# Half of h by seven products in the q/k stage, five probability tiles a head summed by DMA, output by seven products

## The chip, the cores and the metric

One core of a Trainium2 chip runs the kernel. The metric is device time in microseconds (us), the median of timed runs. TensorE (PE) multiplies matrices, VectorE (DVE) and ScalarE (ACT) work on tiles in SBUF and PSUM, GpSimd (POOL) on tiles in SBUF, and the queues of SyncE (SP), ACT and POOL issue transfers to 16 shared DMA engines. Each engine runs its own instructions in a fixed order and waits on semaphores of the others.

## The reference

With S = 2048 tokens, D = 1024, H = 32 heads of 32, F = 3584:

```python
xn = _layernorm(x)
q, k, v = heads(xn @ wqkv)
p = softmax(einsum("bhqd,bhkd->bhqk", q, k) * 32 ** -0.5)
s = merge(einsum("bhqk,bhkd->bhqd", p, v)) @ wo
h = xn @ w1 + b1
g = silu((h * tanh(softplus(h))) @ w2)       # Dense -> Mish -> Dense
return x + s * g
```

All is float32. Products that need its precision are made from two parts of each operand, high and low, in a reduced-precision float format: a product of tiles is three matmuls (high x high, high x low, low x high; `THREE`).

## The kernel before

The program runs in four stages.

1. **v stage.** The rows of x are normalised, transposed and split into high and low (`xc`); PE makes v and stores it in DRAM. Beside it the first 7 of w1's 28 column tiles are split (`w1_early`) and stored in `w1s`.
2. **q/k stage** (L798). Sixteen jobs; each makes one 128-row tile of q and one of k for two of the four 512-column chunks of x, by seven products in place of eight: with sums of quarter blocks of the weights (`w_sum`, on POOL) and of x (`t_half`), each product is 12 matmuls, so a job is 84. Three PSUM banks a job collect the products, DVE adds between them (`after`), ACT and DVE split the results (`out_`), and ACT's queue stores them.
3. **Inner stage.** Four streams are woven on PE by a planner (`Plan`) which, while the program is written, simulates the engines with fixed durations and writes each instruction where it would be ready, by due times (`due`, `key`) and a table of leanings. `s_stream`: scores for the row maxima (L920, one head ahead; DVE reduces them). `t_stream`: for every head h and key tile kt (16 a head, `T` counts them all) four transposed scores (L1007), which ACT turns into a probability tile `p` of 128x2048 by Exp; one of `PS` = 7 buffers. POOL adds the 16 tiles into `z` (L1036), 15 adds a head. `product` (L1054) multiplies groups of 6, 5 and 5 probability tiles with v; these matmuls use PE's columns in four parts, 32 wide, and a stretch of them is called a stay. `norm` sums z over partitions by four such matmuls (`zp`, L1080), inverts it and stores the head in DRAM (`ot`). `h_stream` (L1213): per chunk c and column tile f of w1, 24 matmuls make h, 112 tiles of 128x512 in all; `mish` takes DVE and ACT through the activation; a whole split w1 tile (1 MB) is loaded to one of two buffers for each. `y_stream` (L1303) multiplies the activations with w2 and DVE adds into `yacc`. In the first chunk w1 and w2 are split on the way by ACT and POOL, and kept.
4. **Output** (L1402). 768 matmuls with wo. The first chunk's eight banks are done in two halves, rows k = 0..3 of wo's eight (heads 0 to 15) first. `end` multiplies with silu(y) and adds x.

A tile p is given back when both its add and its product are done (`p_done`).

Of the kernel before, what the change touches and what calls it, by code (L numbers as in the profile page):

```python
# [28 lines left out]
SLOW, UNTIL = 1.25, 700.0  # L29

W2_Q = 0
NS = H * NT
HK = KT // 2

MM, PV = 0.228, 0.86

GROUPS, YB = (6, 5, 5), 2

LEAD, LATE = 5, 4.0

PS, ACTS, W2S, Y0, Y1 = 7, 3, 5, 0.6, 0.17

AHEAD, BEHIND = 1.5, 1
# [9 lines left out]
LEAN = ("11875111088588544715468766661886741604280263056046486663654100588"  # L53
        "24308444562028442608686254255866647666488105044664767708017872000")
# [35 lines left out]
class Plan:  # L90
# [6 lines left out]
    SEM, SWITCH, LAND, RATE = 0.07, (0.25, 0.13), 2.0, 0.25e6  # L97
# [25 lines left out]
    def ready(self, op):  # L123
        when = 0.0
        for o in op.need:
            if o is not None:
                if o.end is None:
                    return None
                when = max(when, o.end + self.SEM)
        if op.late and not self.col:  # L130
            when += op.late
        for name in op.take:
            if not self.rings[name]:
                return None
            when = max(when, min(self.rings[name])[0] + self.SEM)
        return when
# [14 lines left out]
    def do(self, op, when):  # L151
# [11 lines left out]
        else:  # L163
            op.end = start + took
# [66 lines left out]
def body(ctx: ExitStack, tc: tile.TileContext, x, wqkv, wo, w1, b1, w2, out):  # L231
# [17 lines left out]
    w1s = [dram.tile([P, 2, KT, P], F32R, name=f"w1s{i}") for i in range(FT)]  # L249
# [10 lines left out]
    nc.vector.memset(one, 1.0)  # L260
    zero = consts.tile([P, 1], F32, name="zero")
# [38 lines left out]
    def w1_tile(name):  # L300
        return w1p.tile([P, 2, KT, P], F32R, tag="w1", name=name, bufs=2)
# [132 lines left out]
    def split_w(w, raw, job=False):  # L434
        for half in range(2):
            r = slice(half * 4, half * 4 + 4)
            if job:
                nc.gpsimd.tensor_copy(w[:, 0, r], raw[:, r])
            else:
                copy(w[:, 0, r], raw[:, r])  # L440
            low(nc.gpsimd if job else nc.vector, w[:, 1, r], raw[:, r], w[:, 0, r])
# [4 lines left out]
    def w1_early():  # L446
# [3 lines left out]
        if f > 1:  # L450
            move(w1s[f - 2], early_w1.pop(f - 2)[1])
        if f < W1_V:
            raw = vp.tile([P, KT, P], F32, tag="x", name=f"w1e{f}", bufs=XB)
            nc.sync.dma_start(raw, w1[:, f * P:(f + 1) * P].rearrange("(k p) f -> p k f", p=P))
            early_w1[f] = [raw, None]
        if 0 < f <= W1_V:
            raw, _ = early_w1[f - 1]
            early_w1[f - 1][1] = w = w1_tile(f"w1p{f - 1}")
            split_w(w, raw, True)
# [75 lines left out]
    nc.sync.dma_start(bias1, b1.rearrange("(f p) -> p f", p=P))  # L535

    PAIRS = ((2, 3), (0, 1))
    A11, S2, A12, S3, S1, A22, S4 = range(7)
    NQ = 2 * KT
    raws, sums, pieces = {}, {}, {}  # L540

    def q_load(q, tiles, halves=range(2)):
        raws[q] = tiles
        for half in halves:
            col = half * D + q % KT * P
            nc.sync.dma_start(tiles[half], wqkv[:, col:col + P].rearrange("(k p) f -> p k f", p=P))
# [9 lines left out]
    EARLY = {(6, 0): [(7, 0)], (6, 2): [(7, 2)], (6, 4): [(7, 1)], (7, 4): [(8, 0)]}  # L556
# [4 lines left out]
    def piece(n, eng):  # L561
        q, i = SEQ[n]
        if n % 2 == 0:
            pieces["tile"] = w1_tile(f"wq{n // 2}")
        w = pieces[n] = pieces["tile"][:, :, n % 2 * HK:n % 2 * HK + HK]
# [169 lines left out]
    def load_w1(n):  # L735
        w1t[n] = w1_tile(f"w1_{n}")
        move(w1t[n], w1s[n % FT])
# [30 lines left out]
    def ring_of(q):  # L768
        if q < KT + 2:
# [5 lines left out]
    def out_(q, half, chunk_, src):  # L775
        st = sp.tile([P, 2, 512], F32R, tag="qst", name=f"qst{q}_{half}_{chunk_}", bufs=4)
        dst = (qs, ks)[half][q % KT].rearrange("h p n -> p h n")[:, :, chunk_ * 512:(chunk_ + 1) * 512]
# [9 lines left out]
    def product(n):  # L787
        q, i = SEQ[n]
        bank_, e = banks_.setdefault(q, {}), es.setdefault(q, {})
        c0, c1 = PAIRS[q // KT]  # L790
        w, xx = pieces.pop(n), X[q // KT][i]
# [31 lines left out]
    for n, (q, i) in enumerate(SEQ):  # L823
        after = product(n)
        for m in (n + 2, n + 3) if n >= 2 and n % 2 == 0 else ():
            if m >= 7 * NQ:
                continue
            piece(m, nc.vector if q < 11 or m % 2 else nc.gpsimd)
            q_, i_ = SEQ[m]
            if i_ == A22:  # L830
                if q_ == 9:
# [8 lines left out]
            if i_ in ((A12, A22) if q_ else (A22,)) and q_ + 2 < NQ and q_ != 7:  # L840
# [5 lines left out]
        since = n - SEQ.index((KT - 1, 0))  # L846
        for _ in range(T_SPLITS.get(since, 0)):
            t_splits.pop(0)()
        if (q, i) >= (11, 2):
# [5 lines left out]
        if since in (6, 9):  # L855
            q_load(9, ring_of(9), (since == 9,))
        for k in B_LOADS.get(since, ()):
            move(X[1][6][:, :, k], xs[1][:, :, HK + k])
        if i == 0 and q == 10:
            load_head(0)  # L860
        if i == 3 and q == 14:
            load_head(1)
        if i == 5 and q == NQ - 1:
            load_w1(0)
# [13 lines left out]
    for name, n in (("b", 7), ("s", S_B), ("t", T_B), ("d", D_B), ("o", 1), ("p", PS), ("z", 1), ("e", 1), ("r", 1), ("on", 1),  # L878
                    ("act", ACTS), ("w1", 2), ("w2", W2S), ("w2r", 1), ("xc0", 1), ("xc1", 1), ("v", 2), ("mx", 2), ("nm", 2), ("hl", 1),
# [15 lines left out]
    total = 2 * 4 * NS * MM + NC * FT * 48 * MM + NS * PV  # L895
    slot = total / NS

    def due(T):
# [3 lines left out]
        return UNTIL * SLOW + (t - UNTIL) * (total - UNTIL * SLOW) / (total - UNTIL)  # L902
# [33 lines left out]
    def m_chain(h, first, n, maxes, tiles):  # L936
# [23 lines left out]
        def r6(at):  # L960
# [3 lines left out]
            if h == 0:  # L964
                load_w1(1)
# [11 lines left out]
    exps, adds, uses = {}, {}, {}  # L977
# [9 lines left out]
    def p_done(T, by):  # L987

        uses.setdefault(T, []).append(by)
        if len(uses[T]) == 2:  # L990
            plan.give("p", max(o.end for o in uses[T]))

    def t_stream():
        pts = {}
        for T in range(NS):
# [29 lines left out]
            if kt:  # L1025
                add(T, pts)
            if kt in group_of:
                product(T, pts, group_of[kt])

    def add(T, pts):  # L1030
        h, kt = divmod(T, NT)

        def emit(at):
            if kt == 1:
                zs[h] = att.tile([P, S], F32, tag=f"z{at['z']}", name=f"z{h}")
            nc.gpsimd.tensor_tensor(zs[h], pts[T - 1] if kt == 1 else zs[h], pts[T], ALU.add)  # L1036

        def then(o):
            if kt == 1:
                p_done(T - 1, o)  # L1040
            p_done(T, o)
# [519 lines left out]
```

## Time and profile before

| | |
|---|---|
| median of 3 timed runs | 3362.53 us (3361.49 to 3362.98) |
| span of the profiled execution, first to last instruction | 3358.0 us |
| v stage, q/k stage, inner stage, output | 0 to 200, to 521.5, to 3179.1, to 3358 us |
| busy: PE, DVE, ACT, POOL | 3345.8, 2510.8, 2056.5, 2524.7 us |
| granted PE clock | 1.00 |
| DMA | 501.56 MB, 149 GB/s on the mean |

The stages' borders are the first starts of their lines. A row of the groups reads: line, engine, operation, output<-inputs, shapes, count | busy us, mean ns of one | idle time of the engine just before them and what ended it. Matmuls are pipelined, so the duration of one is longer than the distance between two. Times in the timeline count from the start of the span.

### The profile page before, as it was taken

What the parts mean: (1) busy time and instruction counts of PE and PEld (TensorE: products, weight loads), DVE (VectorE), ACT (ScalarE), POOL (GpSimd) and SP (SyncE); (2) the same over time, 40 slices, a digit from 0 to 9 for tenths busy, and PEclk for the clock granted to TensorE, in tenths of its full rate; (3) what the DMA queues carried; (4) which work ended last, traced back from release to release, by engine and by line L of the source; (5) the groups of instructions that cost most, each with busy time, mean ns of one, the idle gap of its engine ahead of it and who ended that gap; (6) DMA issues with size and microseconds to landing.
All of it is one profiled execution on the core that took longest, in us unless ns stands there. A gap on an engine that the chain in (4) does not pass through costs nothing.

```text
span 3358.0 us, 45795 instructions
## 1 busy us (share of the span) xinstructions
PE 3345.8 (100%) x16886; PEld 2458.4 (73%) x16886; DVE 2510.8 (75%) x3987; ACT 2056.5 (61%) x3313; POOL 2524.7 (75%) x750
## 2 busy tenths in 40 slices
PE   9999999999999999999999999999999999999999
PEld 7888887776777677776777677777677777767787
DVE  6665678877877778887888688888787888886542
ACT  5233436676766666666676666666667666667621
POOL 1323546999999887888888988888888898889800
PEclk9999999999999999999999999999999999999999
DMA  7865745454565643343335334333344433433482
GB/s 248 298 204 181 242 146 183 140 184 152 169 191 172 221 126 115 105 122 114 101 117 179 111 101 126 101 112 116 101 151 139 116 106 112 130 108 107 140 304 83
DMA packets 291460, 501.56 MB, mean 149 GB/s; under 512 B 88138, under 2 KB 151114, under 8 KB 269130
## 3 DMA queue, kind: packets, MB, share of 16 engines
q1 hardware_dynamic: 271524, 456.95, 43.8%
q10 hardware_dynamic: 19712, 41.69, 3.3%
q8 instruction: 133, 2.18, 0.3%
q14 instruction: 91, 0.75, 0.1%
HBM read 352.55 MB, written 144.97 MB: 148 GB/s over the span
## 4 chain that ended last, share of the span: by engine, by line
PE 96%; DMA 1%; DVE 1%; POOL 1%; issue 0%; ACT 0%; SPq 0%; ACTq 0%; POOLq 0%; DVEq 0%
PE y L1303 18%; PE h L1213 18%; PE t L1007 14%; PE s L920 13%; PE pv L1054 13%; PE op L1402 5%; PE v L354 5%; PE q_y L798 3%; PE q_z L798 2%; PE q_x L798 2%; PE zp L1080 1%; PE s L700 0%; POOL z L1036 0%; PE pt L423 0%; DMA w2r<-in_B_w_dram 0%
## 5 line engine op out<-in xcount | busy, mean ns | idle before, releaser
L1036 POOL TENSOR_TENSOR z<-z,p 128x2048 f32<-128x2048 f32 x448 | 2067.7, 4615 | 98.0 <-ACT p L285 72.9
L285 ACT ACTIVATE p<-t,zero 128x512 f32<-128x512 f32 x2048 | 1377.1, 690 | 560.1 <-PE t L1007 535.7
L926 DVE TENSOR_REDUCE mx<-s 128x1 f32<-128x512 f32 x1984 | 1322.3, 685 | 382.7 <-PE s L920 371.9
L1303 PE MATMUL y<-w,act 128*128 128x512 f32 x2688 | 920.3, 391 | 0.8 <-DVE yacc L1325 0.5
L1007 PE MATMUL t<-qstack,kstack 128*128 128x512 f32 x2048 | 799.1, 393 | 1.1 <-ACT p L285 0.7
L920 PE MATMUL s<-kstack,qstack 128*128 128x512 f32 x1984 | 772.6, 393 | 0.2 <-ACT p L285 0.2
L1213 PE MATMUL h<-xr,w 128*128 128x512 f32 x2016 | 697.7, 391 | 0.4 <-DMA xr<-xs 0.4
L1303 PEld LDWEIGHTS y<-w,act 128*128 128x128 f32 x2688 | 503.3, 188 | 114.3 <-issue 6.7
L1007 PEld LDWEIGHTS t<-qstack,kstack 128*128 128x128 f32 x2048 | 383.8, 188 | 114.8 <-issue 18.0
L1054 PE MATMUL pv<-p,v 128*32 128x512 f32 x4096 | 459.3, 594 | 0.0
L920 PEld LDWEIGHTS s<-kstack,qstack 128*128 128x128 f32 x1984 | 369.6, 188 | 118.5 <-issue 32.1
L1213 PEld LDWEIGHTS h<-xr,w 128*128 128x128 f32 x2016 | 378.3, 188 | 81.2 <-issue 3.4
L1325 DVE TENSOR_TENSOR yacc<-yacc,y 128x512 f32<-128x512 f32 x416 | 282.7, 680 | 82.6 <-PE y L1303 81.5
L1054 PEld LDWEIGHTS pv<-p,v 128*32 128x32 f32 x4096 | 123.3, 110 | 282.7 <-issue 281.1
L1036 POOL TENSOR_TENSOR z<-p,p 128x2048 f32<-128x2048 f32 x32 | 148.1, 4628 | 185.2 <-PE zp L1080 146.6
L1213 PE MATMUL h<-xc,w 128*128 128x512 f32 x672 | 231.3, 391 | 1.3 <-DMA w<-w1s 1.0
L354 PE MATMUL v<-vw,xc 128*128 128x512 f32 x768 | 179.7, 392 | 1.2 <-ACT xc L288 0.7
L354 PEld LDWEIGHTS v<-vw,xc 128*128 128x128 f32 x768 | 142.7, 188 | 32.0 <-ACT xc L288 1.4
L1213 PEld LDWEIGHTS h<-xc,w 128*128 128x128 f32 x672 | 125.9, 188 | 30.5 <-issue 2.5
L288 ACT ACTIVATE act<-h 128x512 fp32r<-128x512 f32 x112 | 66.6, 595 | 88.2 <-DVE h L1262 87.0
L798 PE MATMUL q_y<-xc,wq 128*128 128x512 f32 x480 | 115.3, 389 | 0.0
L798 PEld LDWEIGHTS q_y<-xc,wq 128*128 128x128 f32 x480 | 90.0, 188 | 18.8
(149 smaller groups left out, 2947.4 us busy)
## 6 DMA issues: line engine op xcount, KB each, us to landing
w<-w1s SPq DMA_DIRECT2D x91, 1024.0 KB, 5.4
w<-w2s SPq DMA_DIRECT2D x168, 512.0 KB, 4.0
w2s<-w SPq DMA_DIRECT2D x56, 512.0 KB, 4.0
qstack<-qs SPq DMA_DIRECT2D x96, 256.0 KB, 6.3
kstack<-ks SPq DMA_DIRECT2D x96, 256.0 KB, 5.8
w1s<-w SPq DMA_DIRECT2D x21, 1024.0 KB, 5.8
qs<-qst ACTq DMA_DIRECT2D x32, 512.0 KB, 4.1
ks<-qst ACTq DMA_DIRECT2D x32, 512.0 KB, 3.7
```

Of the source, the lines that this page charges most:

```text
L285: nc.scalar.activation(out_, in_, fn, bias=zero if bias is None else bias, scale=scale)
L354: nc.tensor.matmul(ps, xc[t // 4][k // HK][:, a, k % HK, (t % 4) * P:(t % 4 + 1) * P], vw[i, k // 2][:, b, k % 2], start=n == 0, stop=n == ...
L798: nc.tensor.matmul(ps, w[:, a, k], xx[:, b, k], start=m == 0 and i in (0, 1, 4), stop=m == 3 * HK - 1, skip_group_check=i not in (0, 1, 4))
L920: nc.tensor.matmul(sp_, qst[h % 3][:, qt * P:(qt + 1) * P], kst[h % 3][:, kc * 512:(kc + 1) * 512], start=True, stop=True)
L926: nc.vector.reduce_max(tiles["mx"][:, qt, kc:kc + 1], tiles[qt, kc], axis=AX.X)
L1007: nc.tensor.matmul(tp, kst[h % 3][:, kt * P:(kt + 1) * P], qst[h % 3][:, c * 512:(c + 1) * 512], start=True, stop=True)
L1036: nc.gpsimd.tensor_tensor(zs[h], pts[T - 1] if kt == 1 else zs[h], pts[T], ALU.add)
L1054: nc.tensor.matmul(pv[h][c * DH:(c + 1) * DH, :], vt[h][:, k, :], pts[T - kt + k][:, c * 512:(c + 1) * 512], start=k == 0, stop=k == NT - 1)
L1213: nc.tensor.matmul(t["h"], w1t[n][:, a, k], xts_[c][k // HK][:, b, k % HK], start=i == 0, stop=i == 3 * KT - 1)
L1303: nc.tensor.matmul(t["y"], acts[n][:, p, s * P:(s + 1) * P], w2t[m_][:, q], start=j == 0 and i == 0, stop=j == YB - 1 and i == 2)
L1325: nc.vector.tensor_tensor(ya, ya, t["y"], ALU.add)
L1402: nc.tensor.matmul(ps[t, dh], ohl[t // 4, k][:, a, s * P:(s + 1) * P], wt[k][:, b, r], start=k == 0 and i == 0, stop=k == KT - 1 and i == 2)
```

## The change

**Half of h.** `MADE` are the odd column tiles of w1, `KEPT` the even ones. In the q/k stage 14 jobs of the new kind "h" stand between the q/k jobs (`JOBS`), seven for each pair of chunks; each makes h for two tiles f of MADE and two chunks by seven products, and stores not h but two tiles for Mish, e = exp(min(h + b, 12)) and (e + 2) e (h + b), in DRAM (`hs`). In the inner stage only KEPT tiles are made by 24 matmuls; for the others `h_load` brings both tiles to one buffer ("hb"), and `mish` starts at the Square. For KEPT tiles the bounded sum is made by an ACT Relu where DVE made it. w1 tiles are loaded in halves (512 KB) to two half buffers.

**Sums of probabilities.** Of a head's 16 tiles, tile 0 is copied to DRAM (`zd`) by SP, tiles 1, 4, 5 and 8 are added to it by accumulating transfers that POOL issues, each after the one before has landed; POOL adds the other eleven into z (ten adds), and one more accumulating transfer adds zd to z. There are two z buffers, 6 probability buffers and groups of 4 tiles. In the last head DVE adds seven tiles into a second sum (`BESIDE`) and no transfer does.

**Output.** Eight jobs of 256 rows, seven products of 12 matmuls each; the sums of quarter blocks of wo (`b_sum`) and their splits are made in the inner stage's end and the first job, those of the attention's rows (`a_sum`) by POOL during the job before.

The core of the diff (`THERE`, `LEAD`, the planner's `LEAN` and the like are numbers for the planner):

```diff
-SLOW, UNTIL = 1.25, 700.0
+SLOW, UNTIL = 0.98, 700.0
+MADE = [f for f in range(FT) if f % 2]
+KEPT = [f for f in range(FT) if f not in MADE]
-GROUPS, YB = (6, 5, 5), 2
+GROUPS, YB = (4, 4, 4, 4), 2
+THERE = (0, 1, 4, 5, 8)
+BESIDE = (3, 6, 9, 11, 13, 14, 15)
-PS, ACTS, W2S, Y0, Y1 = 7, 3, 5, 0.6, 0.17
+PS, ACTS, W2S, Y0, Y1 = 6, 5, 4, 0.6, 0.17
-    SEM, SWITCH, LAND, RATE = 0.07, (0.25, 0.13), 2.0, 0.25e6
+    SEM, SWITCH, LAND, RATE, SUM = 0.07, (0.25, 0.13), 2.0, 0.25e6, 8.5
...
+    JOBS = [("q", t) for t in range(KT)] + [("h", g) for g in range(NM)] * 2 + [("q", t) for t in range(KT)]
...
     def out_(q, half, chunk_, src):
+        if kind == "h":
+            def first():
+                act(num, src, AF.Relu, bias=rest1[:, f:f + 1], scale=-1.0)
+                act(e, num, AF.Exp, bias=twelve, scale=-1.0)
+            def second():
+                nc.vector.scalar_tensor_tensor(src, src, bias1[:, f:f + 1], e, op0=ALU.add, op1=ALU.mult)
+                nc.vector.scalar_tensor_tensor(num, e, 2.0, src, op0=ALU.add, op1=ALU.mult)
...
     def add(T, pts):
-            nc.gpsimd.tensor_tensor(zs[h], pts[T - 1] if kt == 1 else zs[h], pts[T], ALU.add)
+        def there(at):
+            if kt != far[0]:
+                nc.gpsimd.dma_start(zd[h % 2], pts[T], accum_op=ALU.add)
+            else:
+                nc.sync.dma_start(zd[h % 2], pts[T])
+        def here(at):
+            nc.gpsimd.tensor_tensor(zs[h], pts[h * NT + near[0]] if kt == near[1] else zs[h], pts[T], ALU.add)
+        def merge(at):
+            nc.gpsimd.dma_start(zs[h], zd[h % 2], accum_op=ALU.add)
...
     def h_stream():
+            if f in MADE:
+                mish(n, made, ahead)
+                continue
...
     def mish(n, made, t):
-        def d1(at):
-            nc.vector.tensor_scalar(t["e"], t["h"], bias, 12.0, op0=ALU.add, op1=ALU.min)
+        def a0(at):
+            act(t["e"], t["h"], AF.Relu, bias=rest1[:, n % FT:n % FT + 1], scale=-1.0)
...
+    def mm7(j, i):
+        for k in range(HK):
+            for a, b in THREE:
+                nc.tensor.matmul(ps, units[j, i][:, a, k], units[set_, i][b][k] if i == 2 else units[set_, i][b][:, k], start=m == 0 and i in (0, 1, 4),
+                                 stop=m == 3 * HK - 1, skip_group_check=i not in (0, 1, 4))
```

POOL's queue before, at the border of two heads (z_15757 is the sum of the one, z_16535 that of the next; `hl` belongs to the row maxima):

```order
453 L1036 TENSOR_TENSOR z_15757<-z_15757,p_16131 128x2048
454 L296 TENSOR_TENSOR hl<-nm_0_16197,hl 128x16
455 L1036 TENSOR_TENSOR z_15757<-z_15757,p_16172 128x2048
456 L1036 TENSOR_TENSOR z_15757<-z_15757,p_16233 128x2048
457 L1036 TENSOR_TENSOR z_15757<-z_15757,p_16277 128x2048
458 L1036 TENSOR_TENSOR z_15757<-z_15757,p_16327 128x2048
459 L1036 TENSOR_TENSOR z_15757<-z_15757,p_16367 128x2048
460 L1036 TENSOR_TENSOR z_16535<-p_16425,p_16455 128x2048
```

POOL's queue in the change, from one head's merge (into z_17473) through the first part of the next head (z_18177, zd_123):

```order
503 L1094 DMA z_17473<-zd_122 128x2048
504 L1079 DMA zd_123<-p_18060 128x2048
505 L1086 TENSOR_TENSOR z_18177<-p_18115,p_18145 128x2048
506 L1079 DMA zd_123<-p_18198 128x2048
507 L1086 TENSOR_TENSOR z_18177<-z_18177,p_18283 128x2048
508 L1079 DMA zd_123<-p_18248 128x2048
509 L1086 TENSOR_TENSOR z_18177<-z_18177,p_18312 128x2048
510 L1079 DMA zd_123<-p_18342 128x2048
511 L1086 TENSOR_TENSOR z_18177<-z_18177,p_18393 128x2048
512 L1086 TENSOR_TENSOR z_18177<-z_18177,p_18449 128x2048
```

Where adds stood one behind the other, four issues of accumulating transfers now stand among the first adds of a head, and a merge behind its last.

PE's order before, where a head's sum over partitions stands (z_16535 is the sum of the head whose last group of five tiles the pv rows are):

```order
4672 L920 MATMUL s_6_2_17230<-kstack_3336,qstack_3335 128x512
4673 L1054 MATMUL pv_16679<-p_16938,v_16390 32x512 x4
4674 L1054 MATMUL pv_16679<-p_16987,v_16390 32x512 x4
4675 L1054 MATMUL pv_16679<-p_17021,v_16390 32x512 x4
4676 L1054 MATMUL pv_16679<-p_17056,v_16390 32x512 x4
4677 L1054 MATMUL pv_16679<-p_17104,v_16390 32x512 x4
4678 L1080 MATMUL zp_17254<-z_16535,ones 32x512 x4
4679 L920 MATMUL s_6_3_17261<-kstack_3336,qstack_3335 128x512
```

PE's order in the change (z_18177 is the head before; the pv rows are the first group of the next head):

```order
4316 L962 MATMUL s_8_0_18946<-kstack_6694,qstack_6693 128x512
4317 L1126 MATMUL pv_18949<-p_18777,v_18801 32x512 x4
4318 L1126 MATMUL pv_18949<-p_18835,v_18801 32x512 x4
4319 L1126 MATMUL pv_18949<-p_18874,v_18801 32x512 x4
4320 L1126 MATMUL pv_18949<-p_18904,v_18801 32x512 x4
4321 L1151 MATMUL zp_18968<-z_18177,ones 32x512 x4
4322 L962 MATMUL s_8_1_18974<-kstack_6694,qstack_6693 128x512
```

The sum over partitions moved from the end of its own head's products to behind the next head's first group, after the merge.

More of the change, by code (lines that the diff above doesn't have):

```diff
@@ L163, in do @@
         else:
[L164 removed]
+            op.end = start + took + (self.SUM if op.bytes else 0.0)
             took -= self.AHEAD[e]
@@ L1038, in then @@
-        def then(o):
-            if kt == 1:
-                p_done(T - 1, o)
-            p_done(T, o)
-        adds[T] = op("POOL", 4.61, need=exps[T] + (exps[T - 1] if kt == 1 else [adds[T - 1]]), emit=emit,
-                     take=["z"] if kt == 1 else [], then=then)
+        far = THERE if h < H - 1 else ()
+        beside = () if h < H - 1 else BESIDE
+        near = [k for k in range(NT) if k not in far and k not in beside]
+        def there(at):
[3 more added lines that the diff above has]
+                nc.sync.dma_start(zd[h % 2], pts[T])
@@ L1046, in product @@
+        if kt == NT - 1 and far:
+            chain[h] = op("POOL", 0.9, need=[chain[h], dma[h]], emit=merge, bytes_=P * S * 4, key=-1)
     def product(T, pts, size):
@@ new lines, in rest, with keep @@
+            def rest(at, half=half):
+                low(nc.gpsimd, w1t[n, half][:, 1], w1r[n, half], w1t[n, half][:, 0])
+            w1_took[n, half] = w1_last[0] = b = op("SP", 0.1, need=[a, w1_last[0]], emit=raw, take=["w1", "on"], bytes_=P * 512 * 4)
+            a = op("ACT", 0.6, need=[b], emit=high)
+            w1_ops[n, half] = op("POOL", 1.3, need=[a], emit=rest, give=[("on", b)], key=-1)
+        if not early:
+            def keep(at):
+                for half in range(2):
+                    move(w1s[n][:, half], w1t[n, half])
+            w1_kept[n] = op("SP", 0.1, emit=keep, need=[w1_ops[n, 0], w1_ops[n, 1]], bytes_=P * 2048 * 4,
+                            then=lambda o: [w1_done(n, half, o) for half in range(2)])
```

632 lines of the change are left out of this document (381 added, 251 removed).

## The prediction

> **What bounds the kernel now.** I read the busy times by stage first: weights of the v stage to 200 us, the q/k stage to 521.5, the inner stage (attention and both MLP products woven together) to 3179.1, then the output product. Columns: stretch, length, busy us of PE, PEld, DVE, ACT, POOL, granted clock, DMA share, GB/s.
>
> ```profile
> core 0: us, PE busy (x) PEld busy (x) DVE busy (x) ACT busy (x) POOL busy (x), PEclk, DMA share, GB/s
> 200.00:521.50 321.50, 320.71 (x1414) 264.70 (x1413) 211.64 (x315) 115.39 (x210) 119.59 (x86) 1.00 0.60 191
> 521.50:1114.00 592.50, 589.45 (x3008) 424.66 (x3008) 468.95 (x745) 415.26 (x682) 552.03 (x196) 1.00 0.56 173
> 521.50:3179.10 2657.60, 2653.86 (x13792) 1887.01 (x13791) 2097.65 (x3319) 1821.68 (x2907) 2348.29 (x612) 1.00 0.43 133
> 3179.10:3358.00 178.90, 174.26 (x769) 144.01 (x767) 66.73 (x99) 37.16 (x49) 2.41 (x1) 0.99 0.54 197
> ```
>
> PE is without a gap in every stage at full clock. POOL stands next: 552.0 of 592.5 us while the first chunk runs, 2348 of 2658 over the inner stage. The costliest groups say what PE's time is made of, and that it waits for almost nothing (last column).
>
> ```profile
> L1303 PE MATMUL y<-w,act 128*128 128x512 f32 x2688 | 920.3, 391 | 0.8 <-DVE yacc L1325 0.5
> L1007 PE MATMUL t<-qstack,kstack 128*128 128x512 f32 x2048 | 799.1, 393 | 1.1 <-ACT p L285 0.7
> L920 PE MATMUL s<-kstack,qstack 128*128 128x512 f32 x1984 | 772.6, 393 | 0.2 <-ACT p L285 0.2
> L1213 PE MATMUL h<-xr,w 128*128 128x512 f32 x2016 | 697.7, 391 | 0.4 <-DMA xr<-xs 0.4
> L1213 PE MATMUL h<-xc,w 128*128 128x512 f32 x672 | 231.3, 391 | 1.3 <-DMA w<-w1s 1.0
> L1054 PE MATMUL pv<-p,v 128*32 128x512 f32 x4096 | 459.3, 594 | 0.0
> L1402 PE MATMUL op<-wo,xo 128*128 128x512 f32 x384 | 87.4, 389 | 0.0
> L1402 PE MATMUL op<-wo,ohl 128*128 128x512 f32 x384 | 87.4, 389 | 0.0
> ```
>
> So the time is PE's count of matmuls times their pace; only what changes this count, or makes PE wait, counts.
>
> **PE's sum.** A full matmul's duration (391 ns) overlaps the next one, so the pace comes from the stages: 321.5 / 1414 = 0.2274 us in the q/k stage, 174.3 / 768 = 0.2270 in the output. For the inner stage the column work must come off first. PE's timeline around one column stay (start, length):
>
> ```profile
> 1510.91 0.39 PE L1213 MATMUL h<-xr,w 128*128 128x512 f32 x1
> 1511.23 4.50 PE L1054 MATMUL pv<-p,v 128*32 128x512 f32 x40
> 1515.55 1.04 PE L1080 MATMUL zp<-z,ones 128*32 128x512 f32 x8
> 1516.52 0.74 PE L920 MATMUL s<-kstack,qstack 128*128 128x512 f32 x2
> 1517.10 0.40 PE L1007 MATMUL t<-qstack,kstack 128*128 128x512 f32 x1
> ```
>
> Five probability tiles take 4.32 us, 0.864 each, and zp as much as one. From 1510.91 to 1517.10 are 6.19 us; three plain matmuls (0.69) and six such units (5.18) leave 0.32 us for entering and leaving. In the order of the instructions PE has 97 such stays before and 138 in the change (groups of 4 instead of 6, 5, 5 give 32 more, and in about ten heads zp now stands alone). The inner stage's 9408 plain matmuls (2688 + 2048 + 1984 + 2016 + 672) therefore have 2657.6 - 512 x 0.864 - 32 x 0.864 - 97 x 0.32 = 2156.5 us, 0.2292 each.
>
> Taken out: half of h, 1344 x 0.2292 = 308.0 us; 96 of the 768 output matmuls, 21.8. Put in: 14 jobs of 84 in the q/k stage, 1176 x 0.2274 = 267.4; 41 stays, 13.1; one more zp, 0.9. Together -48.4.
>
> **POOL and the engines beside PE.**
>
> ```profile
> L1036 POOL TENSOR_TENSOR z<-z,p 128x2048 f32<-128x2048 f32 x448 | 2067.7, 4615 | 98.0 <-ACT p L285 72.9
> L1036 POOL TENSOR_TENSOR z<-p,p 128x2048 f32<-128x2048 f32 x32 | 148.1, 4628 | 185.2 <-PE zp L1080 146.6
> 1501.90 0.44 SPq L292 DMA_DIRECT2D kstack<-ks  x1
> ```
>
> Fifteen adds a head are 69.2 us. The change leaves ten, 46.2, and gives POOL five issues of an accumulating transfer, which no row shows: at least what an issue costs SP (0.44 us), at most the add that it replaces (4.6). I take 1 us, nearer to the issue, since both only hand over a description. That is 51.5 us of POOL a head, 57 to 66 in the first heads, whose w2 splits stay, against 69 to 78 us of PE work a head counted from the order. Even at 4.6 a head would be 69.5, just under PE's mean of 73. The second z buffer also ends POOL's 146.6 us of waiting for zp.
>
> ```profile
> L1233 DVE TENSOR_SCALAR e<-h,bias 128x512 f32<-128x512 f32 x112 | 83.4, 744 | 24.7 <-PE h L1213 24.1
> L1243 DVE SCALAR_TENSOR_TENSOR h<-h,bias,e 128x512 f32<-128x512 f32 x112 | 84.3, 752 | 12.2 <-ACT e L285 11.5
> L1250 DVE SCALAR_TENSOR_TENSOR h<-e,h 128x512 f32<-128x512 f32 x112 | 76.9, 687 | 0.7
> L285 ACT ACTIVATE e<-e,zero 128x512 f32<-128x512 f32 x112 | 80.5, 719 | 34.2 <-DVE e L1233 33.8
> ```
>
> In the inner stage DVE loses the first group wholly and half of the next two: 83.4 + 42.2 + 38.5 = 164 us, and gains six adds of the last head (four times 0.69 each, 17). It would stand at 1951 of about 2364 us, 82% (79% before); ACT loses 56 Exp and gains 56 Relu, some 1800, 76% (69%). Neither passes PE, but both have less room, so I add 3 us of small waits (0 to 25; nothing in the trace excludes more). In the q/k stage an h job gives ACT eight activations of about 0.72 (5.8 us) where a q job has four copies, and DVE eight operations of 0.69 (5.5) where it has four. With pieces and sums DVE is near 15 of a job's 19.1 us: covered by PE, at nothing; without this cover it would be a few us a job.
>
> **The accumulating transfers.** Each waits for the one before (tiles 0, 1, 4, 5, 8), POOL's queue standing behind that wait; the last, back into z, releases zp. The landing time L of 1 MB isn't shown. Bounds: 1 MB plain, and 2 MB, since an accumulation touches two sources.
>
> ```profile
> w<-w1s SPq DMA_DIRECT2D x91, 1024.0 KB, 5.4
> ys<-yacc SPq DMA_DIRECT2D x4, 2048.0 KB, 10.4
> DMA to landing us min/median/max: 6.1/9.0/13.4
> ```
>
> The third row is for all transfers of ys, the 2 MB stores being the slow ones. I take 10.4 us (the planner in the change counts 8.5), with 5.4 and 13.4 as ends. Between the last t of a head and its zp the order leaves PE 19.9 to 30.9 us of other work (31 heads, mean 25.2). The chain in it is one Exp (0.7), the last add and half of another (6.9) and an issue (1), 8.6 us. So zp is not late up to L = 11.3 in any head, and by some 5 us in all at 13.4: no cost. Between the transfers of tiles 4 and 5 one add stands on POOL in most heads: its wait is L - 5.6, 5 us a head, inside POOL's slack of 15 or more. Tile 0 goes out as a plain copy on SP's queue, which then waits for that tile's Exp with weight loads behind it; the planner lets SP take other ready loads first, and PE's two waits on w1 and xr in the groups above (1.0 and 0.4 us) show how early loads are: nothing.
>
> **The start of the output.** Before, 96 output matmuls on the first heads' rows cover the last head's way through DRAM; now the first product needs all heads.
>
> ```profile
> 3176.39 1.04 PE L1080 MATMUL zp<-z,ones 128*32 128x512 f32 x8
> 3191.97 0.34 SPq L1350 DMA_DIRECT2D or<-ot  x1
> 3196.17 0.69 DVE L296 TENSOR_TENSOR xo<-or,xo 128x512 fp32r<-128x512 f32 x1 [2.25 <-ACT xo L288]
> ```
>
> From zp to the last split operand that way took 3196.9 - 3176.4 = 20.5 us. In the change 15.3 us of y stand between the last zp's end and the first output product: 5 us of waiting (0 if the load follows at once, 10 if POOL's weight splits are late too).
>
> Sum: 3358.0 - 48.4 + 3 + 5 = 3317.6 of span. The median of the timed runs, 3362.5, is 4.5 above the span shown, so **3322 us**. 0.2%, 6.7 us, is about what a measurement of this kernel tells from no change.
>
> **Rivals.**
>
> *Late sums (slower).* If L is far above the rows, zp waits on PE, which is in order. By the order's gaps, waits of zp add up to 30 us at L = 16, 66 at 18, 114 at 20; POOL passes PE's head too. Break-even (40 us) is near 17. At 18: 3322 + 66 = 3388. For it: no row shows an accumulation, and 2 MB took 13.4 at worst. Against: 17 is three times the plain row. Chance 0.15.
>
> *DMA engines full.* The inner stage's share of 0.43 is 1143 us for 353 MB, 3.4 us a tile. Some 150 us of w1 traffic go; one plain and five accumulating tiles a head add 31 x 6 x 3.4 = 632 us if they cost like plain ones, 1160 if double: a share of 69% or 91%. At the latter, loads for which PE has one spare half (w1) land late. With a third of the 112 halves 1 us late: 3322 + 37 = 3359. For the doubling the Trainium skill (Collectives: The Full Stack, The bandwidth ceiling: the fold count and why AG ≠ RS ≠ AR) says that a reducing transfer halves its rate by reading two sources on one ring; no run here shows one yet. Chance 0.12.
>
> *Shared port in the output.* A job has 84 x 0.227 = 19.1 us of PE.
>
> ```profile
> L554 POOL TENSOR_TENSOR ws<-raw,ws 128x512 f32<-128x512 f32 x9 | 13.4, 1486 | 9.8 <-DVE wq L296 9.8
> L296 DVE TENSOR_TENSOR wq<-ws,wq 128x512 fp32r<-128x512 f32 x53 | 42.1, 803 | 20.4 <-ACT wq L288 20.1
> L296 DVE TENSOR_TENSOR xo<-or,xo x8: 679/760/2865, 3164.8 to 3196.2; 128x512 fp32r<-128x512 f32 x8
> ```
>
> DVE's subtraction of two SBUF tiles took 2865 ns beside a POOL add, 679 alone. Ten POOL operations (14.9 us) and ten such of DVE (6.9) a job, if they exclude each other, are 21.8: 2.7 us more than PE, over 8 jobs 22: 3322 + 22 = 3344. Against: in the q/k stage, where both run, DVE's mean is only 803. The Trainium skill (SBUF — State Buffer, Who interferes with whom) states the full exclusion; the one slow row agrees, the mean does not. Chance 0.05.
>
> **Numbers.** The forecast, 3307 (all covers hold, stays cheaper) to 3345, has 0.68. The range reaches over the port and most of the full-DMA case: 3307 to 3364. Faster: 0.68 + 0.05 + 0.05 of the DMA case; same 0.06; slower 0.15 + 0.01.
>
> **What would show it.** Right: q/k stage ending near 789 us, inner stage near 2367 long, output near 153; PE waits under 15 us in all; accumulations landing in 8 to 12 us; POOL near 75% busy. Wrong: PE rows for zp with waits on a transfer (late sums), h rows waiting on w1 loads at a DMA share over 0.85 (full engines), op rows waiting for DVE (port).

## The result, and the profile after

The changed kernel takes 3558.12 us (median of four runs, 3549.63 to 3561.04) against 3362.53 (3361.49 to 3362.98): 1.058 times as long, with a 95% interval of 1.056 to 1.059. The forecast was 3322, its range 3307 to 3364. Its profiled execution spans 3559.1 us, 241.5 more than the sum had given (3317.6).

The busy times by stage of the changed kernel, in the columns of the prediction's first fence (q/k stage, first chunk, the rest of the inner stage, output):

```profile
200.00:793.00 593.00, 588.63 (x2593) 485.54 (x2592) 398.06 (x595) 261.24 (x434) 196.55 (x142) 1.00 0.56 179
793.00:1500.00 707.00, 637.94 (x3136) 423.53 (x3135) 514.41 (x815) 477.26 (x782) 486.43 (x195) 0.96 0.78 199
1500.00:3350.60 1850.60, 1796.45 (x9321) 1224.32 (x9320) 1454.82 (x2284) 1313.35 (x2093) 1237.31 (x387) 0.99 0.80 200
3350.60:3559.00 208.40, 170.00 (x673) 134.01 (x671) 144.75 (x135) 59.96 (x84) 122.14 (x79) 0.91 0.47 167
```

The q/k stage ends where it was forecast (793 for 789). The inner stage is 2557.6 us long instead of 2367, and its DMA share has gone from 0.43 to 0.79. The output takes 208.5 instead of 161.6 (3317.6 less 789 and 2367; its list of signs says 153, which doesn't agree with its sum). Both stages show what the kernel before hardly showed: PE with gaps (123 us of 2557.6, where it had 4 of 2657.6), and a granted clock clearly below 1. No engine beside PE is full: POOL, DVE and ACT all have room. PE's groups, and POOL's issues of the sums:

```profile
L1435 PE MATMUL y<-w,act 128*128 128x512 f32 x2688 | 908.6, 397 | 13.3 <-DMA w<-w2s 5.2
L1047 PE MATMUL t<-qstack,kstack 128*128 128x512 f32 x2048 | 808.2, 401 | 47.9 <-ACT p L296 39.9
L962 PE MATMUL s<-kstack,qstack 128*128 128x512 f32 x1984 | 787.2, 402 | 24.2 <-ACT p L296 23.3
...
L1126 PE MATMUL pv<-p,v 128*32 128x512 f32 x4096 | 476.9, 607 | 20.3 <-DMA v<-vs 20.3
...
L1079 POOL DMA_DIRECT2D zd<-p x124 | 109.5, 883 | 322.4 <-ACT p L296 163.2
```

The last column was near zero before; now t, s, pv and y wait, and each of these matmuls is 6 to 13 ns longer in the mean. t and s wait for Exps. What ACT waits for tells why (waits by releaser: us in total, times, longest):

```profile
ACT w L299 <- DMA more<-in_B_w_dram: 86.1, 33, 8.8
ACT g L296 <- DMA g<-ys: 82.9, 7, 14.7
...
PE t L1047 <- ACT p L296: 39.9, 19, 7.9
...
PE s L962 <- ACT p L296: 23.3, 13, 3.6
...
PE pv L1126 <- DMA v<-vs: 20.3, 5, 5.6
...
PE op_y L1643 <- DVE e L1648: 19.3, 8, 4.8
...
PE zp L1151 <- DMA z<-zd: 8.8, 4, 3.4
```

ACT takes its instructions in order. It stands 86 us in front of copies of raw w2 tiles that haven't landed, 73 of them before 1500 us, with Exps behind them; in the output it stands 83 us in front of Silu, waiting for y. The sums themselves are on time: zp waits 8.8 us in all. One of ACT's waits in the timeline (start, length, and in brackets the idle time before):

```profile
993.90 0.69 ACT L296 ACTIVATE p<-t,zero 128x512 f32<-128x512 f32 x1
1003.41 0.63 ACT L299 ACTIVATE w<-more 128x512 fp32r<-128x512 f32 x1 [8.82 <-DMA more<-in_B_w_dram]
1003.95 2.40 ACT L296 ACTIVATE p<-t,zero 128x512 f32<-128x512 f32 x4
```

and PE's rows at the same place:

```profile
996.42 0.39 PE L1323 MATMUL h<-xc,w 128*128 128x512 f32 x1
1004.67 0.80 PE L1047 MATMUL t<-qstack,kstack 128*128 128x512 f32 x1 [7.86 <-ACT p L296]
...
1009.25 0.63 PE L962 MATMUL s<-kstack,qstack 128*128 128x512 f32 x1
1009.68 0.63 PE L1323 MATMUL h<-xc,w 128*128 128x512 f32 x1
1010.11 0.58 PE L1047 MATMUL t<-qstack,kstack 128*128 128x512 f32 x1
1010.52 0.39 PE L962 MATMUL s<-kstack,qstack 128*128 128x512 f32 x1
1010.75 0.39 PE L1435 MATMUL y<-w,act 128*128 128x512 f32 x1
```

PE loses 7.86 us, and then starts a matmul every 0.43 us instead of 0.23 until 1010.5: the wait is paid for twice. PE's timeline has 29 gaps of over 1.5 us in the inner stage, 17 of them before 1500, 15 of those 17 at Exps; in 14 of the 15, ACT had just stood in front of a raw w2 tile. Last, the queues (packets, MB, share of the sixteen engines' time; q0 is POOL's, q1 SP's) and the landing of the sums:

```profile
q1 hardware_dynamic: 313012, 475.31, 43.6%
q0 software_dynamic: 22320, 162.54, 24.3%
...
zd<-p POOLq DMA_DIRECT2D x124, 1024.0 KB, 9.0
...
z<-zd POOLq DMA_DIRECT2D x31, 1024.0 KB, 11.3
```

### The profile page after: what moved, and what is told of

It is laid out like the page before. It is cut to its first block, busy times and chain, and to the rows that moved or that the text cites. A ratio compares the mean times of both kernels' runs of the same rounds, so it can differ in the third digit from the quotient of the medians.

```text
span 3559.1 us, 46674 instructions
## 1 busy us (share of the span) xinstructions
PE 3389.5 (95%) x16630; PEld 2429.8 (68%) x16630; DVE 2643.0 (74%) x4085; ACT 2193.8 (62%) x3541; POOL 2095.6 (59%) x853
## 3 DMA queue, kind: packets, MB, share of 16 engines
q0 software_dynamic: 22320, 162.54, 24.3%
## 4 chain that ended last, share of the span: by engine, by line
PE 45%; DMA 12%; POOL 3%; ACT 2%; DVE 2%; issue 2%; SPq 1%; POOLq 0%; DVEq 0%; ACTq 0%
PE y L1435 12%; PE pv L1126 9%; PE t L1047 9%; PE s L962 9%; PE h L1323 6%; DMA more<-in_B_w_dram 2%; DMA v<-vs 2%; DMA x<-in_A_x_dram 2%; POOL z L1086 2%; DMA ys<-yacc 1%; DMA z<-zd 1%; ACT p L296 1%; DMA w<-w1s 1%; DVE a L307 1%; PE zp L1151 1%
## 5 line engine op out<-in xcount | busy, mean ns | idle before, releaser
L1086 POOL TENSOR_TENSOR z<-z,p 128x2048 f32<-128x2048 f32 x286 | 1336.2, 4672 | 219.1 <-ACT p L296 201.5
L1435 PE MATMUL y<-w,act 128*128 128x512 f32 x2688 | 908.6, 397 | 13.3 <-DMA w<-w2s 5.2
L1047 PE MATMUL t<-qstack,kstack 128*128 128x512 f32 x2048 | 808.2, 401 | 47.9 <-ACT p L296 39.9
L1126 PE MATMUL pv<-p,v 128*32 128x512 f32 x4096 | 476.9, 607 | 20.3 <-DMA v<-vs 20.3
L1323 PE MATMUL h<-xr,w 128*128 128x512 f32 x1008 | 343.1, 394 | 7.6 <-DMA w<-w1s 6.0
L1079 POOL DMA_DIRECT2D zd<-p x124 | 109.5, 883 | 322.4 <-ACT p L296 163.2
L1323 PEld LDWEIGHTS h<-xr,w 128*128 128x128 f32 x1008 | 189.4, 189 | 51.2 <-DMA w<-w1s 7.9
L839 PE MATMUL q_y<-xc,wq 128*128 128x512 f32 x900 | 216.8, 390 | 3.5 <-DVE e L824 2.7
L839 PEld LDWEIGHTS q_y<-xc,wq 128*128 128x128 f32 x900 | 168.6, 188 | 40.0 <-ACT wq L299 4.0
L839 PE MATMUL q_z<-xc,wq 128*128 128x512 f32 x720 | 173.2, 389 | 0.9 <-DVE e L824 0.8
L839 PE MATMUL q_x<-xc,wq 128*128 128x512 f32 x720 | 172.6, 389 | 0.0
L307 POOL TENSOR_TENSOR w<-more,w 128x512 fp32r<-128x512 f32 x56 | 73.4, 1311 | 155.3 <-ACT w L299 153.1
```

What stands on the lines that cost most here:

```text
L839: nc.tensor.matmul(ps, w[:, a, k], xx[:, b, k], start=m == 0 and i in (0, 1, 4), stop=m == 3 * HK - 1, skip_group_check=i not in (0, 1, 4))
L1047: nc.tensor.matmul(tp, kst[h % 3][:, kt * P:(kt + 1) * P], qst[h % 3][:, c * 512:(c + 1) * 512], start=True, stop=True)
L1079: nc.gpsimd.dma_start(zd[h % 2], pts[T], accum_op=ALU.add)
L1086: nc.gpsimd.tensor_tensor(zs[h], pts[h * NT + near[0]] if kt == near[1] else zs[h], pts[T], ALU.add)
L1126: nc.tensor.matmul(pv[h][c * DH:(c + 1) * DH, :], vt[h][:, k, :], pts[T - kt + k][:, c * 512:(c + 1) * 512], start=k == 0, stop=k == NT - 1)
L1323: nc.tensor.matmul(t["h"], w1t[n, k // HK][:, a, k % HK], xts_[c][k // HK][:, b, k % HK], start=i == 0, stop=i == 3 * KT - 1)
```

## The experiments

Two theories stood at the start. **Traffic**: the bytes of the sums fill the DMA engines, loads land late, and engines that take their instructions in order hold PE up. **Order**: the planner's new order and its shorter rings (one raw w2 tile, two halves of w1, one v, six p) make the waits, whatever the bytes. Times are single runs beside one of the kernel before (3360.4 to 3363.5). Three kernels with the same order in the inner stage (the changed one and two below) had 2557.6, 2550.1 and 2544.9 us there, so differences under 15 us are not read.

**Thin transfers.**

```
-  nc.gpsimd.dma_start(zd[h % 2], pts[T], accum_op=ALU.add)
+  nc.gpsimd.dma_start(zd[h % 2][:, :64], pts[T][:, :64], accum_op=ALU.add)
```

and so for the first copy and the way back into z.

> The changed kernel with the same instructions in the same order on every engine, but each of the six transfers of a head's sum carries 64 of the 2048 columns (1/32 of the bytes), so most of the sum is left out (a 1 is added inside Ln to keep it finite). Traffic theory: the sums' bytes keep the DMA engines full, so loads land late, ACT and PE wait, and PE runs at a lower clock behind each wait. Then the DMA share of the inner stage falls from 0.79 to about 0.5, its length from 2557.6 to 2380-2430 us, PE's clock there from 0.98 to 0.99-1.00, the whole to 3370-3430. Order theory: the waits come from the new order and its shorter rings (one raw w2 tile, one tile of v, one of h) whatever the bytes. Then the share falls as well, but the inner stage stays within 25 us of 2557.6 and the whole within 30 us of 3558.

Measured: 3401.1 us. The inner stage:

```profile
793.00:3191.30 2398.30, 2384.75 (x12464) 1629.14 (x12463) 1967.24 (x3101) 1789.39 (x2876) 1721.01 (x581) 1.00 0.50 135
```

The same instructions in the same order now run in 2398.3 us at full clock. The waits in PE's timeline add up to 11.8 us where they were 121.8, and gaps of over 1.9 us are 1 where they were 25. The bytes cost 159 of the 190.6 us; the order theory keeps at most 31. What the gaps cost behind themselves follows too: PE's busy time fell by 49.6 us, 2.1 for each of the 24 gaps that are gone. The granted clock bears most of it out: in the changed kernel it was at half for 112.6 us of the inner stage, 94 of them with PE busy, which is 47 us lost; with thin transfers it was at half for 6.8 us.

**Plain transfers.** The same edit with `accum_op` left out, whole tiles.

> The changed kernel with the same instructions in the same order, but the four accumulating transfers of a head and the one back into z are plain copies of the same 1 MB (the sum is left out, a 1 is added inside Ln). If the accumulation itself is what costs (a read beside each write), the landing falls from 9.0 to about 5.4 us, the DMA share of the inner stage from 0.79 to 0.60-0.65, and the time goes at least half of the way to that of the kernel with thin transfers. If the bytes alone cost, share and landing stay within a tenth and the time within 30 us of 3558. Order theory: within 30 us of 3558 too, with a lower share.

Measured: 3449.6 us. Inner stage, then the page's queue and landing:

```profile
793.00:3239.00 2446.00, 2397.00 (x12452) 1634.34 (x12451) 1965.77 (x3097) 1789.41 (x2875) 1674.45 (x581) 0.99 0.65 209
```

```profile
q0 software_dynamic: 22320, 162.54, 12.3%
...
zd<-p POOLq DMA_DIRECT2D x124, 1024.0 KB, 5.2
```

At the same megabytes the queue takes half the engines' time: 12.3% of 3447.8 us over 155 transfers is 2.7 us of all sixteen engines for 1 MB; accumulating, 24.3% of 3559.1 is 5.6. So 112 of the 159 us belong to the accumulation, 48 to plain copying. The Trainium skill (Collectives: The Full Stack, The bandwidth ceiling: the fold count and why AG ≠ RS ≠ AR) says of the reducing step of a collective that it has half the rate of a copying one because it reads two sources; the two rows agree with the factor, and no run here shows the reason.

**Two tiles by DMA, and none.** Both with the output's early loads (below).

```
-THERE = (0, 1, 4, 5, 8)
+THERE = (0, 1)          # in the other kernel: ()
```

> The changed kernel with two tiles of a head summed by DMA instead of five (one plain copy, one accumulation, one back into z: five megabytes of reads beside writes in place of eleven), with the output's early loads. Traffic theory: the cost goes with the bytes, so 0.45 of the 152 us that thin transfers took off, some 70 us, is left: inner stage 2440-2480, whole 3420-3460, share 0.6-0.68. Theory of a threshold (nothing costs until the engines are near full): inner 2398-2425, whole 3380-3405. Order theory: near 3540.

> The changed kernel without any transfer in the sums (POOL adds all sixteen tiles of a head again), with the output stage's early loads of the run before. Traffic theory: with the sums' traffic gone (DMA share near 0.5) no load is late, and the inner stage comes out as with thin transfers, 2398 us, plus what POOL now costs: 15 adds of 4.61 us are 69.2 us a head, and with the splits of w1 and w2 about 2350 us of work in 2398, so 0 to 50 us more; the whole 3380-3435. Order theory: the inner stage stays near 2550 and the whole near 3540. A whole under 3355 would say that h by seven products pays once the sums are off the DMA engines.

Measured: 3482.1 and 3446.0 us. Their inner stages:

```profile
793.00:3286.20 2493.20, 2414.94 (x12461) 1633.53 (x12460) 1971.75 (x3101) 1791.54 (x2876) 2071.81 (x581) 0.99 0.60 166
```

```profile
793.00:3250.40 2457.40, 2415.25 (x12459) 1625.32 (x12458) 1970.60 (x3099) 1790.68 (x2875) 2300.20 (x581) 1.00 0.45 129
```

Each inner stage was a little longer than expected. With no transfers POOL is busy for 2300 of 2457 us, and PE's gaps are short (37.3 us in all, 4 above 1.9). But PE is busy for 30 us longer than with thin transfers: the planner's order has 150 stays instead of 138 (4 us), half clock costs 6 us more, and the plain matmuls stand 0.2343 us apart instead of 0.2320 (19). So the sums cost time on either side; how much of it is POOL's load and how much the other order isn't separated here.

Two tiles are worse than plain copies of five although the mean share is lower (0.60 against 0.65). The mean hides how the transfers bunch. With the inner stage divided into pieces of 10 us, the share is 0.95 or more in 83 of 255 pieces of the changed kernel, in 59 of 249 with two tiles, in 46 of 244 with plain copies, in 20 of 239 with thin ones, and in 20 of 265 in the kernel before. The inner stages of the first four have their lengths in the same order (2558, 2493, 2446, 2398). That the full pieces set the price is not shown by this alone, since POOL is fuller with two tiles and the order another.

**Sums by DMA without h by seven products** (also with the early loads).

```
-MADE = [f for f in range(FT) if f % 2]
+MADE = []
```

> The changed kernel with no h made in the q/k stage (all 28 tiles by the inner stage's 24 matmuls, as before), but the sums by DMA and the output by seven products, with its early loads. Without any waits of the inner stage: 200 + 321.5 + 2657.6 + 13 for the stays + 193 of output + 4.5 = 3390 us. If the transfers of the sums are harmful by themselves, the loads are late here too (DMA share over 0.7) and the whole is 3430-3520; if they hurt only together with the h loads and the shorter heads (69-78 us against 83), it is 3385-3410.

Measured: 3673.7 us, above both expectations. Where PE waited in it, and its inner stage:

```profile
PE h L1323 <- DMA w<-w1s: 71.8, 31, 6.0
```

```profile
521.50:3480.40 2958.90, 2795.23 (x13802) 1907.39 (x13801) 2054.65 (x3211) 1877.74 (x3015) 1753.42 (x609) 0.97 0.72 186
```

Late loads come without h by seven products too. But this kernel also differs from the one before in w1's ring: all 28 tiles come through two halves of 512 KB, where two whole tiles stood, and h waits for them. So it doesn't tell the sums from the shorter ring. Of the 288 us above 2671, 158 are waits, and 64 are lower clock (half clock for 129 us of busy PE). Some 53 of the rest are matmuls that start a little late, too little to count as a wait: plain ones at full clock stand 0.2348 us apart in the mean, where 0.2292 was taken.

**Is it the queue, or the order?** Three tries on the kernel with the early loads (3538.2). The first moves tile 0 of each head from SP's queue to ACT's:

```
-                nc.sync.dma_start(zd[h % 2], pts[T])
+                nc.scalar.dma_start(zd[h % 2], pts[T])
```

> The changed kernel with the output's early loads (3538.2 us), in which tile 0 of each head goes out by ACT's DMA queue instead of SP's; every other instruction stands where it stood. If SP standing behind that tile's Exps (95.8 us in 20 waits, one issue held for 15.4 us) is what makes the loads behind it late, the inner stage falls from 2550 to 2480-2525 us and the whole to 3465-3515. If the loads are late because the engines are full, whatever queue asks for them, the whole stays within 15 us of 3538.

Measured: 3576.0 us, 38 more, which neither side expected. My guess that SP stood in its own way was wrong: with SP free of the copy PE waited longer for v (41.7 us in 8 waits, against 17.2 without this edit).

```profile
PE pv L1126 <- DMA v<-vs: 41.7, 8, 7.9
```

That copies which go out sooner take time from the loads fits this, but is only argued. The others give the planner longer landing times:

```
-    SEM, SWITCH, LAND, RATE, SUM = 0.07, (0.25, 0.13), 2.0, 0.25e6, 8.5
+    SEM, SWITCH, LAND, RATE, SUM = 0.07, (0.25, 0.13), 3.5, 0.25e6, 10.5   # and 2.0, 10.5
```

> The changed kernel with the output's early loads (3538.2 us), in which the planner counts 10.5 us instead of 8.5 for a sum's landing and 3.5 us instead of 2.0 for a load's, so that it writes another order of the same work. If the waits come from an order written for transfers that land sooner than they do, PE's idle time in the inner stage falls from 122 us to 40-70 and the whole to 3440-3490. If the rings (one raw w2 tile, two halves of w1, one v) are too short for these transfers in any order, or the order only moves the waits, the whole stays within 25 us of 3538.

> As the run before, but the planner counts the longer time for the sums alone (10.5 us, loads 2.0 as they were). If late loads are what stops PE, as in the traces so far (Exps behind raw w2, pv on v, h on w1), this alone brings little: within 25 us of 3538. If late sums holding the p tiles are the matter after all, it brings as much as both together.

Measured: 3566.4 and 3571.2 us, 28 and 33 above 3538, so a little outside the 25 expected; PE's waits in the inner stage 118.3 and 126.3 us, as before. The orders differ, the waits only move (in the first: h on w1 22.5 us, pv on v 8.1). In a fourth version the planner also booked the bytes of POOL's transfers, twice, on the queue that it simulates; there it came to a point where nothing could go on, so there is no kernel of it. Two other orders are no proof that none is better, but fewer bytes stay the only thing that took the waits away.

**Raw w2 copied by POOL**, to free ACT of these loads.

```
-            copy(w2t[m][:, 0], w2r[m])
+            nc.gpsimd.tensor_copy(w2t[m][:, 0], w2r[m])
```

> The changed kernel, in which the high half of each raw w2 tile (56 of them, in the first chunk) is copied by POOL instead of ACT, so that ACT's queue no longer stands behind raw w2 loads (86.1 us in 33 waits). If these waits of ACT are what holds back the Exps, and so PE, in the first chunk, the stretch from 793 to about 1500 us gets 30-60 us shorter and the whole 3500-3530. If the late loads merely move on (POOL then stands in front of them and its sums, zp and the p tiles come late instead), the whole stays within 15 us of 3558 or gets slower.

Measured: 3578.1 us. PE's y matmuls in it:

```profile
L1435 PE MATMUL y<-w,act 128*128 128x512 f32 x2688 | 897.5, 401 | 55.7 <-POOL w L1261 27.6 <-POOL w L307 10.3 <-DMA w<-w2s 9.9
```

t waits 11.1 us for Exps instead of 39.9, and y waits 55.7 us instead of 13.3: the late load has found another engine to stop. PE's waits in the inner stage are 121.9 us in all, as before.

**The price of a gap**, by itself, in a kernel that computes nothing of the reference.

```
+    for ops in (1, 2, 3, 4, 6, 10, 16):
+        for _ in range(3):
+            gap(ops)      # a chain of DVE operations that PE waits for
+            run(90)       # plain matmuls
```

> Nothing of the reference is computed: runs of 90 plain matmuls (128x512) with waits of PE between them, made by chains of 1, 2, 3, 4, 6, 10 and 16 DVE operations (three of each), then single-operation waits after every 10, 20 and 40 matmuls. Theory that a wait costs twice: behind a wait of 1.9 us and more PE runs at half rate for some microseconds (12 matmuls took 4.80 us after 1.87 us and 5.16 after 4.81, against 2.88), so the first 10-12 matmuls behind each gap take 0.4-0.45 us each, about 2 us lost per gap, whatever its length, and frequent short gaps keep the rate low. Rival: the low clock comes from the load on the whole chip (DMA, all engines), not from the gap; then every run goes on at 0.227 us a matmul right behind its gap.

PE's timeline (start, length of the run, and the gap before it):

```profile
209.46 20.70 PE L45 MATMUL bank<-a,w 128*128 128x512 f32 x90 [1.71 <-DVE a L52]
232.33 20.69 PE L45 MATMUL bank<-a,w 128*128 128x512 f32 x90 [2.17 <-DVE a L52]
255.19 22.31 PE L45 MATMUL bank<-a,w 128*128 128x512 f32 x90 [2.17 <-DVE a L52]
...
352.67 20.71 PE L45 MATMUL bank<-a,w 128*128 128x512 f32 x90 [3.09 <-DVE a L52]
378.32 22.30 PE L45 MATMUL bank<-a,w 128*128 128x512 f32 x90 [4.94 <-DVE a L52]
...
524.08 22.95 PE L45 MATMUL bank<-a,w 128*128 128x512 f32 x90 [7.71 <-DVE a L52]
547.82 2.58 PE L45 MATMUL bank<-a,w 128*128 128x512 f32 x10 [0.78 <-DVE a L50]
```

Up to 1.7 us a gap costs only itself. At 2.17 two of three runs are 1.6 us longer, at 3.09 none, at 4.94 all (1.6 to 1.8), at 7.7 by 2.1 to 2.25. So the rival falls, since next to nothing else ran on the chip; but half of the theory falls too: gaps of 0.78 us after every ten matmuls, a quarter of the time, don't lower the rate, and length alone doesn't decide near 2 to 3 us.

The granted clock of this trace shows what decides. Behind these gaps it is low only at one half, in stretches of 3.41 us or twice or three times that, and all of them begin on one grid of 3.41 us. Here are pieces of that grid (PE, PEld, DVE, POOL, clock, DMA): two at a gap of 2.17 us, three at one of 3.09.

```profile
252.41:255.82 3.41, 1.24 (x6) 0.73 (x5) 1.97 (x4) 0.00 (x0) 1.00 0.00 0
255.82:259.23 3.41, 3.41 (x10) 2.64 (x9) 0.00 (x0) 0.00 (x0) 0.50 0.00 0
...
300.19:303.61 3.42, 1.79 (x8) 1.13 (x7) 1.52 (x3) 0.00 (x0) 1.00 0.00 0
303.61:307.02 3.41, 1.95 (x8) 1.61 (x9) 1.30 (x4) 0.00 (x0) 1.00 0.00 0
307.02:310.43 3.41, 3.41 (x16) 2.82 (x15) 0.00 (x0) 0.00 (x0) 1.00 0.00 0
```

The gap of 2.17 us lies wholly in one piece, and the next piece runs at half clock. The gap of 3.09 us is divided by a border into 1.63 and 1.46 us, and nothing follows. So it is through all the gaps of this run: no piece at full clock with up to 1.90 us of idle PE was followed by a low one, and every piece with 1.97 us or more was. The three gaps of 3.09 us are not three chances, since equal runs put them at nearly the same place of the grid. The Trainium skill (TensorE: Matmul & The Clock Gate, What's actually happening) has the clock halved by a free-running window of 3.4 us; the trace agrees with the window and with the half, but here some 2 us of idle time within one window were enough.

**The output: y earlier.**

```
-            if i == 1:
-                out_load(j)
+            if j == 0 and i == 1:
+                out_load(0)
+            if i == 5 and nxt <= last:
+                out_load(nxt)
```

> The changed kernel, in which the output stage loads y and x of a job at the fifth product of the job before instead of the second product of its own (the first job as it was). If ACT's in-order wait for y (82.9 us in 7 waits) is what makes the split operands and DVE's e late for PE, the output stage falls from 208.5 to 165-180 us and the whole to 3515-3535, with no op_y wait on DVE e once a job. If DVE and POOL exclude each other there (21.8 us a job against 19.1 of PE), or the clock stays low by itself, the output stage stays above 195 us and the whole within 15 us of 3558.

Measured: 3538.2 us; the output stage 193.3, so 15.2 of its 47 us of excess, half of the least that was expected. Silu's waits are gone, op_y's waits on DVE are still there (11.5 us), and DVE's subtractions are slow:

```profile
L307 DVE TENSOR_TENSOR a<-araw,a 128x512 fp32r<-128x512 f32 x40 | 56.2, 1423 | 0.0
```

**The output with less of POOL beside it.**

```
-        eng.tensor_tensor(out_, a, b, how)
+        n = 64 if eng is nc.gpsimd else 512
+        eng.tensor_tensor(out_[:, :n], a[:, :n], b[:, :n], how)
```

> The changed kernel with the output's early loads (output stage 193.3 us from the first output matmul, 3343.1, to the end), in which POOL's eight multiplications and additions of a job at the end of the output's tiles take 64 of the 512 columns (the rest of those columns is left out); what POOL sums for the next job stays. If DVE's subtractions beside them (1423 ns in the mean where 684 is usual) are what still makes DVE's e late for PE once a job, the output stage falls from 193.3 to 178-186 us and op_y's waits on DVE e from 11.5 to under 4 us. If the first job's operands and the end are all that is left of the excess over 158 us, the output stage stays within 4 us of 193.

Measured: 3515.2 us. The same DVE group and the output stage:

```profile
L307 DVE TENSOR_TENSOR a<-araw,a 128x512 fp32r<-128x512 f32 x40 | 42.5, 1079 | 0.0
```

```profile
3337.90:3513.40 175.50, 159.69 (x673) 128.97 (x672) 118.87 (x135) 60.66 (x84) 73.62 (x79) 0.96 0.55 198
```

17.8 us less, a little more than expected, and op_y waits 0.4 us for DVE's e. Two things went at once: DVE's subtractions are 13.7 us shorter in all, and DVE's own waits for POOL's products fell from 20.7 to 1.3 us; the run doesn't tell them apart. What is left, 13.9 above 161.6, is mostly the first job: its operands hold PE up for 9.4 us (5 were forecast), at a lower clock behind it.

## Why the prediction was wrong

**The count of PE's work was right, its pace a little low.** The q/k stage came out at 593 us against 589. With thin transfers the inner stage has 2384.8 us of busy PE against a forecast of 2364 without waits: plain matmuls stood 0.2320 us apart in the mean, not 0.2292, and that alone is some 22 us of the 48 to be gained. The accumulations landed at 9.0 us (10.4 was taken, 8 to 12 the test), an issue cost POOL 0.88 us (1.0), ACT and DVE were busy for 1791 and 1969 us (1800 and 1951), POOL for 1724 (75% of the forecast length is 1775). By its own terms POOL's sums a head are 51.2 and 69.2 us, not 51.5 and 69.5; nothing hangs on it.

**The step that failed** is "so I add 3 us of small waits", together with "no cost" for the transfers and "nothing" for the weight loads in SP's queue. I followed the sums along their own chain, from the last Exp to zp, and there they were on time. For the loads I took PE's waits on w1 and xr in the kernel before (1.0 and 0.4 us) as a sign of how early they are; but those were measured without the sums' bytes on the engines. With the bytes the inner stage is 159 us longer: 110 of waits, and 50 of slower PE behind them (47 by the granted clock, where thin transfers have 3), for which the sum had no term at all.

**The rival of full engines was the right mechanism, four times too cheap.** It priced 37 us, a third of the w1 halves 1 us late. The loads that hurt most were others, raw w2 with one buffer in front of ACT's Exps and v with one buffer; they came several us late, not one; and it had 0.12. It also asked for a share of 0.85 to 0.91, and a mean of 0.79 was enough, with a third of the 10 us pieces at 0.95 and more. That an accumulation costs twice was written there, and measured: 5.6 us of all engines a megabyte against 2.7. The plain price was taken too high (3.4), the doubling was right.

**The output came 47 us above its forecast.** 15.2 are y's load, asked for one product before Silu needs it, which the prediction didn't look at; 17.8 are POOL's work beside DVE, which it had as a rival at 22 us with a chance of 0.05; the rest is mostly the first job. That rival was priced down by a mean over a whole stage and called one row slow. The eight subtractions behind its last row say more: the four beside POOL took 0.83, 1.41, 2.62 and 2.87 us, the four alone 0.68 to 0.69.

**The rival of late sums didn't come**: zp waited 8.8 us, in four places.

Put together, even free transfers and both repairs of the output would give 793 + 2398.3 + 175.5 = 3366.8 us of span, against 3358.0 before: the 48.4 us saved on PE are used up by the 8 us of waits that were forecast and by 31 more in the inner stage, 13.9 in the output and 4 in the q/k stage. This sum is from separate runs and was not run as one kernel. No kernel tried beats the one before.

## What to carry to other kernels

A transfer that is on time for its own reader can still be the dearest thing in a stage: price its bytes at the loads with the fewest buffers, and at the in-order engine that stands in front of each of them. A mean share of the DMA engines below 1 is not room: look at it in pieces as short as a load takes. Price a wait of PE above some 2 us as its length and 2 us more. Work taken off an engine that was covered (POOL here) buys nothing unless the place that it goes to is covered as well; look at where every sum, load and copy will stand before counting the matmuls that are saved.

## What the runs showed of the hardware

- Behind a gap PE ran at half clock, 0.43 us a matmul instead of 0.23, in stretches of 3.41 us or a multiple on a fixed grid, for 1.6 to 2.25 us of loss. In the run of gaps it followed whenever 1.97 us or more of one piece of the grid were idle, and never at 1.90 or less.
- An accumulating 1 MB took 5.6 us of all sixteen engines in the mean of 155 transfers, 124 of them from SBUF to DRAM, which landed in 9.0 us; plain ones 2.7, and 5.2 to landing. POOL's issue took 0.88 us accumulating and 0.57 plain.
- SP's rows for the issue of tile 0's plain copy last 0.32 us at the least, 3.4 in the median and up to 15.4. With 1/32 of the bytes they last 5.0 in the median and up to 10.7, so it is not the engines' load that makes them long. From ACT's queue the same issue took 0.33 each time.
- DVE's subtraction of two SBUF tiles in the output took 1.65 us in the mean in the 29 cases that ran beside a POOL operation, 0.69 in the 11 that didn't; over all 40 it took 1.42, and 1.08 with most of the columns of POOL's operations gone.
